# Attention and mixture-of-experts on one core: the dense branch moved into the attention stage, TensorE's order written by hand

## The chip, the cores and the metric

The kernel runs on one core of a Trainium2 chip. The metric is device time in microseconds (us) of one execution, from the first to the last instruction with what lies around it; lower is better. TensorE (PE) runs the matmuls, VectorE (DVE) and ScalarE (ACT) read and write the tiles, GpSimd (POOL) computes squares and issues the DMAs of v, of the weights and of all gathers and scatters, SyncE (SP) issues the other DMAs.

## The reference

```python
# attention: q, k, v of 8 batches x 12 heads x 448 positions x 64
q_n, k_n = rmsnorm(q, g_q), rmsnorm(k, g_k)
attn = softmax(q_n @ k_n.T / 8)          # per head
x = (attn @ v) as (3584 tokens, 768)
# mixture of experts on x, D = 768, E = 8, F = 512
y_dense = relu(x @ w1_dense) @ w2_dense
expert_idx = argmax(x @ w_gate); gate_w = softmax(x @ w_gate)[expert_idx]
y_moe[token] = gate_w * (relu(x @ w1[e]) @ w2[e])   # e = expert_idx[token]
out = y_dense + y_moe
```

## The kernel before

The work has three stages.

**Attention.** A unit of work is a pair of heads (48 pairs, 6 for each batch of 448 tokens). A group of two pairs is loaded at a time: q and k by SP (L132), v by POOL (L140). For each pair POOL squares q and k (L151), DVE sums the squares (L152), ACT makes the reciprocal root (L158, L159) and DVE multiplies (L167). TensorE transposes the result (L177) and DVE copies it out of PSUM (L182, L184). Then TensorE makes the scores of both heads in four score tiles, one for each quarter of the keys (L193), ACT takes the exponentials (L195), TensorE multiplies them with v (L206, 32 matmuls per pair), DVE divides by the sums (L214, L219), TensorE transposes the 448 x 128 result (L227) and ACT copies it to `xT` (L229). After a batch's sixth pair `route` makes the gate logits (L238), the choice of expert on DVE, and two DMAs of the token rows to the DRAM tensor `x_rows` (L258, L259). Meanwhile the weights of the dense branch (`wd`) and of all eight experts (`we`) come in through POOL's queue (L114, L115).

**Routing.** Two matmuls count the tokens of each expert, a chain of DVE instructions (L312 to L390) turns the counts into a sorted list of 35 tiles of 128 slots, each tile of one expert, with a chain of 32 matmuls (L370) in the middle.

**Experts.** For each of the 35 tiles POOL gathers its rows (L397), TensorE transposes them (L407, to `xp`), multiplies them with the expert's first matrix (L414, to `he`) and with the dense branch's first (L420, to `hd`), transposes the expert's hidden values (L426), and adds dense (L432) and expert (L436) products into `yp`; DVE copies `yp` to `ys` (L440) and POOL scatters the rows to `out` (L441).

The order of each engine's instructions is set by a list scheduler that sees the program as written and its data dependences; a tile pool with n buffers lets a producer run n tiles ahead. Matrix tiles in PSUM: two score tiles of two banks, one `av` of two banks, two `tr` of one.

Of the kernel before, what the change touches and what calls it, by code (L numbers as in the profile page):

```python
# [17 lines left out]
def kernel(  # L18
# [89 lines left out]
    nc.gpsimd.dma_start(wgb, moe_w_gate.rearrange("(ko p) e -> p ko e", p=P))  # L108
# [4 lines left out]
    def load_weights(dst1, dst2, s1, s2):  # L113
        nc.gpsimd.dma_start(dst1, s1.rearrange("(ko p) f -> p ko f", p=P))  # L114
        nc.gpsimd.dma_start(dst2, s2.rearrange("(fo p) d -> p fo d", p=P))  # L115

    def load_expert(dst, e):
        load_weights(dst[:, 0].rearrange("p (ko f) -> p ko f", f=F),
                     dst[:, 1].rearrange("p (fo d) -> p fo d", d=Dm), moe_w1[e], moe_w2[e])

    with tc.tile_pool(name="a_ld", bufs=3) as ld, \
         tc.tile_pool(name="a_sb", bufs=2) as sb, \
         tc.tile_pool(name="a_sc", bufs=2, space=bass.MemoryType.PSUM) as scp, \
         tc.tile_pool(name="a_av", bufs=1, space=bass.MemoryType.PSUM) as avp, \
         tc.tile_pool(name="a_tr", bufs=2, space=bass.MemoryType.PSUM) as trp:
        xin, ssqs, rs, xn, qkT, exs, vas, xnats, xTs = {}, {}, {}, {}, {}, {}, {}, {}, {}

        def load(g):
            b, h0 = divmod(g * GP * 2, H)
            for name, src in (("q", q), ("k", k)):  # L130
                t = ld.tile([SC, 2 * GP, JJ * D], F32, tag="x" + name)
                nc.sync.dma_start(  # L132
                    t, src[b, h0:h0 + 2 * GP].rearrange("h (p j) d -> p h (j d)", j=JJ))
                xin[name, g] = t
            ssqs[g] = sb.tile([SC, 2, 2 * GP * JJ], F32, tag="ssq", name="ssq")

        def load_v(g):
            b, h0 = divmod(g * GP * 2, H)
            vr = ld.tile([SC, 2 * GP, JJ * D], BF16, tag="vr", bufs=2)
            nc.gpsimd.dma_start(vr, v[b, h0:h0 + 2 * GP].rearrange("h (p j) d -> p h (j d)", j=JJ))  # L140
            va = ld.tile([SC, 2 * GP, JJ, D + 2], BF16, tag="va")
            nc.vector.memset(va[:, :, :, D:], 1.0)
            nc.vector.tensor_copy(va[:, :, :, :D], vr.rearrange("p h (j d) -> p h j d", d=D))  # L143
            vas[g] = va

        def squares(t):
            g, i = divmod(t, GP)
            for n, name in enumerate("qk"):
# [5 lines left out]
                    sq.rearrange("p h (j d) -> p (h j) d", d=D), AX.X, ALU.add)  # L154

        def rnorm(g):
            r = sb.tile([SC, 2, 2 * GP * JJ], F32, tag="r", name="r")
            nc.scalar.activation(r, ssqs[g], AF.Ln, bias=eps_t[:SC], scale=1.0 / D)  # L158
            nc.scalar.activation(r, r, AF.Exp, scale=-0.5)  # L159
            rs[g] = r  # L160

        def normalise(t):
            g, i = divmod(t, GP)
            for n, name in enumerate("qk"):
# [8 lines left out]
        def transposes(t):  # L173
            for name in "qk":
                ps = trp.tile([P, S], BF16, tag="tr")
                for j in range(JJ):
                    nc.tensor.transpose(ps[:, j * SC:(j + 1) * SC],  # L177
                                        xn[name, t][:, j].rearrange("p h d -> p (h d)"),
                                        ident[:SC, :SC])
                y = sb.tile([P, S], BF16, tag="T" + name)  # L180
                if name == "q":
                    nc.vector.tensor_scalar(y, ps, gqk, None, op0=ALU.mult)  # L182
                else:
                    nc.vector.tensor_copy(y, ps)  # L184
                qkT[name, t] = y

        def scores(t, j):
            if j == 0:
                exs[t] = sb.tile([SC, JJ, 2, S], BF16, tag="ex", name="ex", bufs=2)
# [7 lines left out]
        av = {}  # L197

        def attend(t, part):
            b, pr = divmod(t, NPR)  # L200
            if part == 0:
                av[t] = avp.tile([P, 2, 512], F32, tag="av", name="av")
            hh, m0 = divmod(part * 2, 4)
            for mi in (m0, m0 + 1):
                for j in range(JJ):
                    nc.tensor.matmul(av[t][:, hh, mi * De:(mi + 1) * De],  # L206
                                     exs[t][:, j, hh, QC[mi]:QC[mi] + P],
                                     vas[t // GP][:, 2 * (pr % GP) + hh, j, :De],
                                     start=(j == 0), stop=(j == JJ - 1))

        def divide(t):
            a4 = av[t][:, :, :4 * De].rearrange("p h (m e) -> p h m e", e=De)
            inv = sb.tile([P, 2, 4, 1], F32, tag="inv")
            nc.vector.reciprocal(inv, a4[:, :, :, D:])  # L214
            b, pr = divmod(t, NPR)
            if pr == 0:
                xnats[b] = sb.tile([P, 4, RW], BF16, tag="xa", name="xa", bufs=2)
                xTs[b] = sb.tile([P, NPR, S], BF16, tag="xT", name="xT", bufs=1)
            nc.vector.tensor_mul(  # L219
# [55 lines left out]
        for t in range(2 * GP):  # L275
            norm_ahead(t)
# [205 lines left out]
```

## Time and profile before

| | us |
|---|---|
| median of 3 runs | 606.62 |
| lowest, highest | 598.64, 606.91 |
| the profiled execution | 599.36 |
| its span in the trace | 597.7 |

The profiled execution is 1.2% below the median. The span can be cut by the stage: attention until about 318 us, routing until the first expert tile at about 354 us, the experts until 592 us. Shares of an engine over the whole span mix these stages.

### The profile page before, as it was taken

To read this page: it belongs to the slowest core of one execution; us is meant where nothing else is said; L and a number is where in the kernel's file an instruction comes from. 1 tells how busy PE (TensorE), PEld (TensorE's weight loads), DVE (VectorE), ACT (ScalarE), POOL (GpSimd) and SP (SyncE) were. 2 spreads that over 40 slices of the span, in tenths; PEclk is the share of its full clock that TensorE was granted. 3 is DMA by queue.
4 is the path that set the end of the run, shared out by engine and by line. 5 is a ranking of instruction groups with operands and counts; after the bars stand their busy time and mean duration, and the time that the engine had idled before them with its cause. 6 is when DMAs were issued, how large, how long until landed. Compare 5 with 4: busy or idle time off the path is not lost.

```text
span 597.7 us, 11804 instructions
## 1 busy us (share of the span) xinstructions
PE 443.1 (74%) x4682; PEld 294.6 (49%) x4682; DVE 311.6 (52%) x666; ACT 247.4 (41%) x367; POOL 205.7 (34%) x223
## 2 busy tenths in 40 slices
PE   0558766679986697689781058888889888888895
PEld 0335444445554465456450046556656565555663
DVE  4589976678778768776645513223232322223231
ACT  0447774566676677667780002111121122111220
POOL 5567654336344333542000022222322233222321
PEclk9998985575587858855995559999999999999999
DMA  8999999993654365443101012222122122222210
GB/s 174 222 157 237 239 250 225 230 237 80 148 130 125 82 137 139 78 124 78 47 3 47 0 41 82 71 80 80 64 86 91 65 81 93 90 80 73 81 63 1
DMA packets 55253, 65.89 MB, mean 110 GB/s; under 512 B 4365, under 2 KB 51725, under 8 KB 55200
## 3 DMA queue, kind: packets, MB, share of 16 engines
q0 software_dynamic: 28768, 37.59, 30.2%
q1 hardware_dynamic: 26432, 27.54, 16.5%
q8 instruction: 39, 0.64, 0.4%
q14 instruction: 14, 0.11, 0.1%
HBM read 68.27 MB, written 19.28 MB: 146 GB/s over the span
## 4 chain that ended last, share of the span: by engine, by line
DMA 31%; issue 26%; PE 17%; DVE 15%; POOL 4%; ACT 4%; SPq 1%; POOLq 0%; DVEq 0%; ACTq 0%
DMA out_dram<-ys,dest 16%; DMA vr<-in_v_dram 7%; PE av L206 7%; DMA t<-in_k_dram 5%; PE ps L193 5%; DVE y L167 4%; ACT ex L195 4%; POOL sq L151 3%; PE ps L177 2%; DVE xa L219 2%; DMA t<-in_q_dram 2%; DVE ssq L152 2%; PE ps L227 2%; DVE va L143 1%; POOL xg L397 1%
## 5 line engine op out<-in xcount | busy, mean ns | idle before, releaser
L195 ACT ACTIVATE ex<-ps 112x896 bf16<-112x896 f32 x192 | 168.9, 918 | 67.7 <-PE ps L193 66.5
L151 POOL TENSOR_TENSOR sq<-t 112x512 f32<-112x512 f32 x96 | 101.5, 1074 | 109.1 <-DMA t<-in_q_dram 56.3
L193 PE MATMUL ps<-y 64*112 64x448 bf16 x384 | 98.3, 493 | 41.9 <-DVE y L184 25.9
L206 PEld LDWEIGHTS <-ex 112*128 112x128 bf16 x1536 | 73.6, 114 | 70.8 <-issue 40.4
L206 PE MATMUL av<-va,ex 112*128 112x65 bf16 x1536 | 93.8, 220 | 18.1 <-DVE xa L219 18.0
L416 ACT ACTIVATE hs<-he,xg 128x512 bf16<-128x512 f32 x35 | 24.1, 687 | 183.0 <-PE he L414 183.0
L441 POOL DMA_INDIRECT out_dram<-ys,dest x35 | 35.5, 1016 | 158.7 <-DVE ys L440 158.7
L167 DVE TENSOR_TENSOR y<-t,r 112x512 bf16<-112x512 f32 x96 | 78.7, 843 | 1.6 <-ACT r L159 1.6
L152 DVE TENSOR_REDUCE ssq<-sq 112x8 f32<-112x512 f32 x96 | 62.9, 675 | 26.8 <-POOL sq L151 26.8
L440 DVE COPY ys<-yp 128x768 f32<-128x768 f32 x35 | 33.5, 958 | 77.4 <-PE yp L436 77.4
L432 PE MATMUL yp<-wd,hdT 128*128 128x384 bf16 x280 | 51.6, 327 | 25.8 <-ACT hdT L423 20.0
L397 POOL DMA_INDIRECT xg<-x_rows,row x35 | 34.2, 977 | 86.3 <-DVE dest L390 70.6
L193 PEld LDWEIGHTS <-y 64*112 64x112 bf16 x384 | 30.3, 148 | 64.3 <-DVE y L184 29.4
L177 PE MATMUL ps<-ident,y 112*128 112x112 bf16 x384 | 40.1, 262 | 26.9 <-DVE y L167 24.6
L428 DVE COPY heT<-hp 128x512 bf16<-128x512 bf16 x35 | 14.9, 425 | 85.1 <-PE xp L407 71.5
L420 PEld LDWEIGHTS <-wd 128*128 128x128 bf16 x840 | 51.1, 99 | 8.6 <-issue 0.6
L420 PE MATMUL hd<-xT,wd 128*128 128x128 bf16 x840 | 53.9, 222 | 0.0
L414 PE MATMUL he<-we,xT 128*128 x210 | 52.3, 386 | 0.8 <-DVE xT L409 0.8
L436 PE MATMUL yp<-we,heT 128*128 x280 | 51.2, 326 | 0.0
L432 PEld LDWEIGHTS <-hdT 128*128 128x128 bf16 x280 | 24.5, 98 | 45.3 <-ACT hdT L423 24.6
L177 PEld LDWEIGHTS <-y 112*128 112x128 bf16 x384 | 30.1, 124 | 29.7 <-DVE y L167 25.3
L423 ACT ACTIVATE hdT<-hd 128x512 bf16<-128x512 f32 x35 | 20.9, 597 | 43.3 <-PE xp L407 38.9
(95 smaller groups left out, 392.8 us busy)
## 6 DMA issues: line engine op xcount, KB each, us to landing
we<-in_moe_w_dram POOLq DMA_DIRECT2D x16, 768.0 KB, 29.1
t<-in_q_dram SPq DMA_DIRECT2D x24, 448.0 KB, 5.9
t<-in_k_dram SPq DMA_DIRECT2D x24, 448.0 KB, 7.0
vr<-in_v_dram POOLq DMA_DIRECT2D x24, 224.0 KB, 6.7
x_rows<-xa SPq DMA_DIRECT2D x8, 577.5 KB, 3.7
wd<-in_moe_w_dense_dram POOLq DMA_DIRECT2D x2, 768.0 KB, 10.1
x_rows<-xa SPq DMA_DIRECT2D x8, 96.2 KB, 3.6
xg<-x_rows,row POOLq DMA_INDIRECT x35, 3.1
```

What stands on the lines that cost most here:

```text
L151: nc.gpsimd.tensor_mul(sq, x, x)
L152: nc.vector.tensor_reduce(ssqs[g][:, n, 2 * i * JJ:(2 * i + 2) * JJ], sq.rearrange("p h (j d) -> p (h j) d", d=D), AX.X, ALU.add)
L167: nc.vector.tensor_mul(y.rearrange("p j h d -> p h j d"), x.rearrange("p h (j d) -> p h j d", d=D), rs[g][:, n, 2 * i * JJ:(2 * i + 2) * J ...
L177: nc.tensor.transpose(ps[:, j * SC:(j + 1) * SC], xn[name, t][:, j].rearrange("p h d -> p (h d)"), ident[:SC, :SC])
L193: nc.tensor.matmul(ps[:, hh, :S], qkT["k", t][d0:d0 + D, j * SC:(j + 1) * SC], qkT["q", t][d0:d0 + D, :], start=True, stop=True)
L195: nc.scalar.activation(exs[t][:, j], ps[:, :, :S], AF.Exp, scale=scale)
L206: nc.tensor.matmul(av[t][:, hh, mi * De:(mi + 1) * De], exs[t][:, j, hh, QC[mi]:QC[mi] + P], vas[t // GP][:, 2 * (pr % GP) + hh, j, :De], ...
L397: nc.gpsimd.indirect_dma_start(out=xg, out_offset=None, in_=xd, in_offset=bass.IndirectOffsetOnAxis(ap=row[:, t:t + 1], axis=0))
L414: nc.tensor.matmul(he, xT[:, kk], we[:, bass.ds(ereg, 1), 0, kk * F:(kk + 1) * F].rearrange("p o f -> p (o f)"), start=(kk == 0), stop=(kk ...
L420: nc.tensor.matmul(hd[:, ff], wd1[:, kk, ff * P:(ff + 1) * P], xT[:, kk], start=(kk == 0), stop=(kk == KD - 1))
L432: nc.tensor.matmul(yp[:, dd, :HD], hdT[:, ff], wd2[:, ff, dd * HD:(dd + 1) * HD], start=(ff == 0), stop=False)
L436: nc.tensor.matmul(yp[:, dd, :HD], heT[:, ff], we[:, bass.ds(ereg, 1), 1, ff * Dm + dd * HD:ff * Dm + (dd + 1) * HD] .rearrange("p o f -> ...
```

## The change

Five things change together.

- The **dense branch** leaves the expert tiles. It is computed batch by batch inside the attention loop from `xT`, one batch behind: `dense1` (24 matmuls of 448 columns, ACT's relu after each six) and `dense2` (32 matmuls of 384 columns, copied out by ACT and DVE in turn), cut into 28 pieces that are dealt out over the four quarters of a pair. Its result is written by SP to DRAM beside the token row: the tensor `records` has rows of 1153 floats where `x_rows` had 385. An expert tile gathers the whole record and adds the dense part when it copies `yp` out.
- TensorE's instructions in the attention loop stay in the **order of the program** (`manual_schedule`): one score tile of a quarter, then a transposition or one head of the product with v, then dense pieces. `attend` works on one head, with its own division.
- All PSUM tiles but the scores share one pool of four one-bank buffers.
- q, k and v are loaded three groups ahead, and the weights are a list of jobs issued along the pairs.
- The **expert loop** is written as a software pipeline in TensorE's program order, with two PSUM buffers for `he`, gathers four tiles ahead, and `yp` in one buffer.

```diff
-    xd = nc.dram_tensor("x_rows", (N, RW // 2), F32).ap()
+    RC = RW // 2 + Dm
+    rec = nc.dram_tensor("records", (N, RC), F32).ap()
...
+         tc.tile_pool(name="a_wk", bufs=4, space=bass.MemoryType.PSUM) as wkp:
...
+        def attend(t, hh):
...
+            av = wkp.tile([P, 4, De], F32, tag="wk", name="av")
+            for mi in range(4):
...
+            inv = sb.tile([P, 4, 1], F32, tag="inv")
+            nc.vector.reciprocal(inv, av[:, :, D:])
+            h = 2 * pr + hh
+            nc.vector.tensor_mul(xnats[b][:, :, h * D:(h + 1) * D], av[:, :, :D],
+                                 inv.to_broadcast([P, 4, D]))
...
+        def dense1(b, ff, part, n=3):
+            if part == 0:
+                if ff == 0:
+                    hTs[b] = sb.tile([P, FT, S], BF16, tag="hT", name="hT", bufs=1)
+                ffs[0] = wkp.tile([P, S], F32, tag="wk", name="ff")
+            for kk in range(part * KD // n, (part + 1) * KD // n):
+                nc.tensor.matmul(ffs[0], wd1[:, kk, ff * P:(ff + 1) * P], xTs[b][:, kk],
+                                 start=(kk == 0), stop=(kk == KD - 1))
+            if part == n - 1:
+                nc.scalar.activation(hTs[b][:, ff], ffs[0], AF.Relu)
+
+        def dense2(b, j, dd, part, n=2):
+            if part == 0:
+                if dd == 0:
+                    ffs[1] = sb.tile([SC, 2, Dm // 2], F32, tag="ys", name="ys")
+                ffs[0] = wkp.tile([SC, Dm // 2], F32, tag="wk", name="ff")
+            for ff in range(part * FT // n, (part + 1) * FT // n):
+                nc.tensor.matmul(ffs[0], hTs[b][:, ff, j * SC:(j + 1) * SC],
+                                 wd2[:, ff, dd * Dm // 2:(dd + 1) * Dm // 2],
+                                 start=(ff == 0), stop=(ff == FT - 1))
+            if part == n - 1:
+                if dd == 0:
+                    nc.scalar.copy(ffs[1][:, dd], ffs[0])
+                else:
+                    nc.vector.tensor_copy(ffs[1][:, dd], ffs[0])
+                    r0 = b * S + j * SC
+                    nc.sync.dma_start(rec[r0:r0 + SC, RW // 2:],
+                                      ffs[1].rearrange("p a d -> p (a d)"))
...
+        with tc.manual_schedule(engines={mybir.EngineType.PE}):
...
+            for t in range(NT + NPR):
...
+                for i in range(4):
+                    if t + 1 < NT:
+                        scores(t + 1, i)
+                    if i % 2 == 0:
+                        if t + 2 < NT:
+                            transposes(t + 2, "qk"[i // 2])
+                        if i == 2 and 0 < t <= NT:
+                            xtrans(t - 1)
+                    elif t < NT:
+                        attend(t, i // 2)
+                    dense(t, i)
...
+            ys = sb.tile([P, 2, HD], F32, tag="ys")
+            nc.vector.tensor_add(ys, yp[:, :, :HD],
+                                 xgs[t][:, RW // 2:].rearrange("p (a d) -> p a d", a=2))
...
+        with tc.manual_schedule(engines={mybir.EngineType.PE}):
+            for t in range(2):
+                xtrans(t)
+            gemm1(0)
+            htrans(0)
+            for t in range(NTL):
+                if t + 4 < NTL:
+                    gather(t + 4)
+                if t + 1 < NTL:
+                    gemm1(t + 1)
+                if t + 2 < NTL:
+                    xtrans(t + 2)
+                gemm2(t)
+                if t + 1 < NTL:
+                    htrans(t + 1)
```

In the middle of the attention stage, TensorE goes from the last product with v of one quarter to a transposition of the divided result (`xa`) and to the next score before:

```order
L206 LDWEIGHTS ex
L206 MATMUL av<-va,ex 128x65
L227 LDWEIGHTS xa
L227 MATMUL ps<-ident,xa 128x128
```

and at the same kind of place now, with `hT` the hidden values of the dense branch of the batch before and `wd_128` its second matrix:

```order
L211 LDWEIGHTS ex
L211 MATMUL av<-va,ex 128x65
L276 LDWEIGHTS hT
L276 MATMUL ff<-wd_128,hT 112x384
L276 LDWEIGHTS hT
L276 MATMUL ff<-wd_128,hT 112x384
L198 LDWEIGHTS y
L198 MATMUL ps<-y 112x448
```

Dense matmuls now stand between the product with v and the next scores.

In the expert stage, POOL's queue before, with the semaphores that each instruction waits for (`DMASW` are those of POOL's own DMAs, in rotation):

```order
L441 DMA out_dram<-ys,dest 3584x768 [waits DMASW1_49,DVE_49]
L397 DMA xg<-x_rows,row 128x385 [waits DMASW6_49,Activation_49]
L441 DMA out_dram<-ys,dest 3584x768 [waits DMASW3_49,DVE_49]
L397 DMA xg<-x_rows,row 128x385 [waits DMASW0_49,Activation_49]
L441 DMA out_dram<-ys,dest 3584x768 [waits DMASW5_49,DVE_49]
```

and now:

```order
L487 DMA out_dram<-ys,dest 3584x768 [waits DMASW6_49,DVE_49]
L441 DMA xg<-records,row 128x1153 [waits DMASW1_49,Activation_49]
L487 DMA out_dram<-ys,dest 3584x768 [waits DMASW0_49,DVE_49]
L441 DMA xg<-records,row 128x1153 [waits DMASW3_49,Activation_49]
L487 DMA out_dram<-ys,dest 3584x768 [waits DMASW2_49,DVE_49]
```

The order is the same: scatters and gathers take turns, the gathered rows are three times as long, and a scatter waits for the landing of the scatter before it (`DMASW0`, then `DMASW2`, is the semaphore of the scatter two rows up).

On DVE, between the last batch's routing and the first instruction of the routing stage (`tot`), before:

```order
L256 RECIPROCAL xa<-sm 128x4
L305 MEMSET oh 64x8x4
L312 COPY tot<-tp 128x256
L314 MEMSET onef 128x32
L317 SCALAR_TENSOR_TENSOR incl<-onef,tot 128x32 x8
```

and now:

```order
L253 RECIPROCAL xa<-sm 128x4
L349 MEMSET oh 64x8x4
L283 COPY ys<-ff 112x384 x4
L356 COPY tot<-tp 128x256
L358 MEMSET onef 128x32
L361 SCALAR_TENSOR_TENSOR incl<-onef,tot 128x32 x8
```

The last batch's dense results now stand ahead of the routing stage.

## Rows read from the trace of the kernel before

**Rows 1.** Busy time by stage: window, length, each engine's busy (instructions), clock, DMA, GB/s.

```profile
0.00:130.00 130.00, 78.18 (x874) 49.62 (x874) 95.17 (x214) 70.31 (x104) 72.61 (x89) 0.83 1.12 219
130.00:300.00 170.00, 136.89 (x1607) 89.55 (x1607) 125.38 (x288) 119.84 (x177) 63.35 (x64) 0.70 0.47 108
318.00:354.00 36.00, 4.11 (x39) 3.55 (x40) 16.98 (x39) 0.00 (x0) 2.99 (x3) 0.50 0.12 36
358.00:592.00 234.00, 206.99 (x1934) 140.54 (x1931) 66.90 (x104) 44.27 (x69) 65.31 (x66) 1.00 0.22 75
```

**Rows 2.** TensorE in order of time, one expert tile: start, length, instruction.

```profile
444.88 1.50 PE L420 MATMUL hd<-xT,wd 128*128 128x128 bf16 x24
446.22 0.39 PE L426 MATMUL hp<-ident,hs 128*128 128x128 bf16 x4
446.44 0.50 PE L407 MATMUL xp<-ident,xg 128*128 128x128 bf16 x6
447.77 1.48 PE L432 MATMUL yp<-wd,hdT 128*128 128x384 bf16 x8 [0.83 <-issue]
449.08 1.46 PE L436 MATMUL yp<-we,heT 128*128 x8
450.38 1.46 PE L414 MATMUL he<-we,xT 128*128 x6
```

**Rows 3.** POOL in order of time: the scatters of two neighbouring tiles.

```profile
445.02 1.02 POOL L441 DMA_INDIRECT out_dram<-ys,dest  x1 [4.49 <-DVE ys L440]
451.81 1.02 POOL L441 DMA_INDIRECT out_dram<-ys,dest  x1 [4.50 <-DVE ys L440]
```

**Rows 4.** The scatters' tile view: from issue to landing.

```profile
DMA to landing us min/median/max: 2.1/3.1/3.1
```

**Rows 5.** TensorE in order of time, one pair to the next at the lower clock.

```profile
262.46 1.06 PE L206 MATMUL av<-va,ex 112*128 112x65 bf16 x16
268.16 1.06 PE L206 MATMUL av<-va,ex 112*128 112x65 bf16 x16 [0.17 <-DVE xa L219]
```

**Rows 6.** The same at the higher clock, late, with no preparation of q and k left.

```profile
304.83 0.64 PE L206 MATMUL av<-va,ex 112*128 112x65 bf16 x15
...
308.14 0.40 PE L193 MATMUL ps<-y 64*112 64x448 bf16 x2 [0.32 <-ACT ex L195]
308.52 0.68 PE L206 MATMUL av<-va,ex 112*128 112x65 bf16 x16
```

**Rows 7.** L206 alone by window: 32 matmuls are one pair; then clock, DMA, GB/s.

```profile
0.00:130.00 130.00, 31.27 (x496) 0.83 1.12 219
130.00:300.00 170.00, 56.53 (x912) 0.70 0.47 108
192.00:205.00 13.00, 3.57 (x74) 1.00 0.41 89
230.00:243.00 13.00, 3.50 (x72) 1.00 0.43 90
```

**Rows 8.** Busy time as in Rows 1, in two stretches of one clock each.

```profile
254.00:284.00 30.00, 27.48 (x276) 18.00 (x272) 21.86 (x53) 20.66 (x30) 10.43 (x11) 0.50 0.42 101
230.00:243.00 13.00, 8.37 (x119) 5.24 (x118) 9.83 (x24) 9.48 (x14) 5.62 (x6) 1.00 0.43 90
```

**Rows 9.** The chain that ended last, between attention and routing: start, length, what.

```profile
313.53 0.70 DVE xa L219
...
317.65 3.66 DMA x_rows<-xa
```

**Rows 10.** TensorE, the first expert tile's first product, at the lower clock.

```profile
353.70 2.72 PE L414 MATMUL he<-we,xT 128*128 x6 [0.82 <-DVE xT L409]
```

**Rows 11.** DMA of the first 130 us: volume, and `x_rows`: count, KB each, us to landing.

```profile
DMA packets 29221, 28.49 MB, mean 219 GB/s; under 512 B 1962, under 2 KB 29211, under 8 KB 29211
...
x_rows<-xa SPq DMA_DIRECT2D x2, 577.5 KB, 11.0
```

**Rows 12.** The page's costliest groups: busy, mean ns of one, idle before.

```profile
L440 DVE COPY ys<-yp 128x768 f32<-128x768 f32 x35 | 33.5, 958 | 77.4 <-PE yp L436 77.4
...
L423 ACT ACTIVATE hdT<-hd 128x512 bf16<-128x512 f32 x35 | 20.9, 597 | 43.3 <-PE xp L407 38.9
```

More of the change, by code (lines that the diff above doesn't have):

```diff
@@ L128, in load @@
         def load(g):
+            if g * GP >= NT:
+                return
             b, h0 = divmod(g * GP * 2, H)
+            parts = ((0, 2), (2, 4)) if g == 0 else ((0, 2 * GP),)
             for name, src in (("q", q), ("k", k)):
[L131 to L134, printed above, removed]
+                xin[name, g] = ld.tile([SC, 2 * GP, JJ * D], F32, tag="x" + name, name="x" + name)
@@ L135, in load, with values @@
+            for a, z in parts:
+                for name, src in (("q", q), ("k", k)):
+                    nc.sync.dma_start(
+                        xin[name, g][:, a:z],
+                        src[b, h0 + a:h0 + z].rearrange("h (p j) d -> p h (j d)", j=JJ))
+            vr = ld.tile([SC, 2 * GP, JJ * D], BF16, tag="vr")
+            nc.gpsimd.dma_start(vr, v[b, h0:h0 + 2 * GP].rearrange("h (p j) d -> p h (j d)", j=JJ))
+            vrs[g] = vr
             ssqs[g] = sb.tile([SC, 2, 2 * GP * JJ], F32, tag="ssq", name="ssq")
[L137 to L140, printed above, removed]
+        def values(g):
@@ L154, in squares, with normalise @@
                     sq.rearrange("p h (j d) -> p (h j) d", d=D), AX.X, ALU.add)
[L156 to L162, printed above, removed]
+            if i == GP - 1 and "k" in names:
+                r = sb.tile([SC, 2, 2 * GP * JJ], F32, tag="r", name="r")
+                nc.scalar.activation(r, ssqs[g], AF.Ln, bias=eps_t[:SC], scale=1.0 / D)
+                nc.scalar.activation(r, r, AF.Exp, scale=-0.5)
+                rs[g] = r
+        def normalise(t, names="qk"):
             g, i = divmod(t, GP)
-            for n, name in enumerate("qk"):
+            for name in names:
+                n = "qk".index(name)
                 x = xin[name, g][:, 2 * i:2 * i + 2, :]
@@ new lines, with dense @@
+        ffs = [None, None]
+        PIECES = [(dense1, ff, p) for ff in range(FT) for p in range(3)] + \
+                 [(dense2, j, dd, p) for j in range(JJ) for dd in range(2) for p in range(2)]
+        NSL = 4 * NPR - 2
+        def dense(t, i):
+            b, pr = divmod(t, NPR)
+            n = 4 * pr + i - 2
+            if b > 0 and n >= 0:
+                for f, *args in PIECES[n * len(PIECES) // NSL:(n + 1) * len(PIECES) // NSL]:
+                    f(b - 1, *args)
+        with tc.manual_schedule(engines={mybir.EngineType.PE}):
+            for g in range(3):
+                load(g)
+            for job in wjobs[:3]:
+                nc.gpsimd.dma_start(*job)
+            for t in range(2 * GP):
+                squares(t)
+            values(0)
+            for t in range(3):
+                normalise(t)
+            for t in range(2):
+                transposes(t, "q")
+                transposes(t, "k")
@@ L422, in ffn @@
-            hdT = sb.tile([P, FT, P], BF16, tag="hdT")
-            nc.scalar.activation(hdT, hd, AF.Relu)
-            hp = ps1.tile([P, FT, P], BF16, tag="tr")
-            for ff in range(FT):
-                nc.tensor.transpose(hp[:, ff], hs[:, ff * P:(ff + 1) * P], ident)
-            heT = sb.tile([P, FT, P], BF16, tag="heT")
-            nc.vector.tensor_copy(heT, hp)
+                nc.tensor.matmul(he, xTs[t][:, kk],
+                                 we[:, bass.ds(eregs[t], 1), 0, kk * F:(kk + 1) * F]
+                                 .rearrange("p o f -> p (o f)"),
+                                 start=(kk == 0), stop=(kk == KD - 1))
@@ L444, in ffn @@
                 bounds_check=N - 1, oob_is_err=False)
[L446 removed]
+        eregs = {}
+        for t in range(4):
             gather(t)
[L448 to L451 removed]
+        with tc.manual_schedule(engines={mybir.EngineType.PE}):
+            for t in range(2):
+                xtrans(t)
[11 more added lines that the diff above has]
+                    htrans(t + 1)
 _INS = ['q', 'k', 'v', 'g_q', 'g_k', 'moe_w_gate', 'moe_w1_dense', 'moe_w2_dense', 'moe_w1', 'moe_w2']
```

192 lines of the change are left out of this document (76 added, 116 removed).

## The prediction

> **What bounds the kernel now.** I read the busy time by stage first, since the shares over the whole span mix three different limits [rows 1]. In the expert stage TensorE is busy 207.0 of 234 us at the full clock, and no other engine comes near 30%: that stage is TensorE's. In the attention stage it changes at about 130 us. Until then the DMA share stands at 1.12, which is as full as it gets, and 28.49 MB move at 219 GB/s [rows 1, 11]: all expert weights come in here beside q, k and v, and only 496/32 = 15.5 pairs get done, 8 us each [rows 7]. From 130 to 300 us the DMA share is 0.47; 912/32 = 28.5 pairs take 170 us, 5.96 us each, with TensorE busy 136.9, DVE 125.4 and ACT 119.8 us, at a mean clock of 0.70 [rows 1, 7].
>
> The 0.70 is a mixture of the two levels, 1.2 and 2.4 GHz. At 1.2 GHz one pair follows the other in 268.16 - 262.46 = 5.70 us with TensorE almost without a gap [rows 5], and in one such stretch of 30 us it is busy 27.48 [rows 8]: TensorE is the bound. At 2.4 GHz it needs 308.52 - 304.83 - 0.32 of wait = 3.37 us for a pair [rows 6]; yet with the preparation of later pairs going on beside it, pairs take 13/(74/32) = 5.6 and 13/(72/32) = 5.8 us, and TensorE is busy only 8.37 of 13 us, DVE 9.83, ACT 9.48 [rows 7, 8]: a chain of waits through all engines, with none of them full. Routing is a chain of 36 us in which TensorE does next to nothing [rows 1].
>
> **The expert stage.** A tile's period is 451.81 - 445.02 = 6.79 us [rows 3]. From start to start on TensorE [rows 2] the removed parts are L420 (446.22 - 444.88 = 1.34 us), L432 (449.08 - 447.77 = 1.31 us) and the wait of 0.83 us ahead of it for the dense hidden values. What stays is the first product, 1.29 us (as L414 before L420: 6 x 512 columns at L436's rate, 8 x 384 in 450.38 - 449.08 = 1.30), L436 at 1.30, four transpositions in 446.44 - 446.22 = 0.22 and six in 0.33: 3.14 us. The new order puts each product's successor far enough away: ACT's relu and copy (0.6 us each by L423) and DVE's copy of `xT` have a product of 1.3 us to hide behind. The one `yp` buffer must be emptied by the add (0.96 us, as L440 [rows 12]) within the 0.22 + 1.29 + 0.33 = 1.84 us until the next L436, which holds with 0.9 us to spare; if DVE came that much late, the excess would be paid in every tile.
>
> The next in line is POOL's scatter. It waits for the landing of the one before, which comes 3.1 us after its issue, and 2.1 us for a tile without tokens [rows 4]; before, 6.79 us hid that, now it is the neighbour of 3.14. With the wait's own reaction I take 3.2 to 3.3 for that chain. POOL itself has a gather and a scatter of 1.0 us each, which fit. The gather grows from 1540 to 4612 bytes a row; a scatter carries 393 KB in the 1.0 us by which a full one is later than an empty one, so a gather of 590 KB costs about 1.5 us of transfer. Both together are 2.5 us of DMA in a period, which still fits. TensorE and the scatters can trip over each other, so I take 3.4 us for a tile, between 3.2 and 4.2 (a scatter that shares the engines with the larger gather lands up to 1 us later). The stage changes by 35 x (3.4 - 6.79) = -119 us (-126 to -91).
>
> **The attention stage.** TensorE gets per batch 24 matmuls of 448 columns and 32 of 384. At L420's rate, 1.34/24 = 0.056 us for 128 columns, one of the first costs 0.195 us; at L432's, 1.31/8 = 0.164. That is 4.7 + 5.2 = 9.9 us a batch, 1.65 a pair, at 2.4 GHz, and double that at 1.2 (L414's six in 2.51 us on the first tile [rows 10], against 1.29). A pair then needs 3.37 + 1.65 = 5.0 us of TensorE at the high clock and 5.7 + 3.2 = 8.9 at the low one. ACT does 119.84/28.5 = 4.2 us a pair now and gets four relus (0.5 to 0.6 us, L423 [rows 12]) and four copies (about 0.5) per batch: +0.7. DVE does 4.4 and gets four copies a batch (+0.3) and a second reciprocal with the division cut in two (about +0.3): 5.0. So all three come to 4.9 to 5.0 us. That they were only some 75% full before came from waits for loads and for each other; loads three groups ahead and the interleaving take part of those away. I take 5.7 us a pair at the high clock (5.2 if the waits vanish), and for the clock a seventh of the time at 1.2 GHz, so 6.2 us a pair: 28.5 x (6.2 - 5.96) = +7 us. The last four pairs, which took 3.7 us [rows 6], now need the 5.0 of TensorE: +5. SP's added writes of the dense rows are 11 MB over the whole stage, where the DMA share after 130 us is 0.47: hidden; ahead of 130 us only one or two batches' rows (1.4 MB each, 6 us at 219 GB/s) come on top, and there the pairs wait for the same weights and loads as before, so I leave that phase at its 130 us, plus or minus 8. Cutting the division, sharing PSUM buffers and the finer loads cost nothing that is not in these sums.
>
> The clock is the largest unknown. The trace shows both: TensorE busy 27.48 of 30 us and still at 1.2 GHz [rows 8], and 234 us at 2.4 GHz under dense products [rows 1]. I take a seventh because the dense products fill the gaps after which it fell. The Trainium skill, "TensorE: Matmul & The Clock Gate", section "What's actually happening", says that the slow clock is the default and that recent activity releases it. Taken by itself that would leave almost no time at 1.2 GHz and a pair at 5.7, which gives 488 us for the whole; the 30 us of [rows 8] speak against it.
>
> **Between the stages.** The last batch's dense branch has no pairs left to hide in. Its 9.9 us of TensorE follow the last routing logits, its last results pass through DVE ahead of `tot`, and a row buffer waits for a DMA of 3.7 us. Before, `tot` waited 3.66 us for `x_rows` [rows 9], which this takes the place of: +10 us (+8, or +20 at the low clock). The routing chain itself stays.
>
> **Sum** on the profiled execution's 599.4 us: -119 + 12 + 10 = **502 us**. The median of the runs is 1.2% above that execution; I don't add it.
>
> **The rivals.**
> - *The low clock keeps its share.* With 60% of the time at 1.2 GHz, as the mean of 0.70 says for now, a pair takes 0.4 x 5.7 + 0.6 x 8.9 = 7.6 us, +40: about 543. For it: the clock stayed low under 92% busy. Against it: dense products replace the gaps. Chance 0.13.
> - *The scatter chain lengthens.* DMAs did land late when the engines were full: `x_rows` took 11.0 us in the first 130 us [rows 11], against 3.66 later [rows 9]. With 4.3 us a tile, +31: 533. Against it: 2.5 us of transfer in 3.4. The Trainium skill, "DMA: Bandwidth & Descriptors", section "Latency and other measured facts", gives HBM's latency as 0.2 us on average and 2 us at high load; by that the estimate for a tile would be some 5 us and for the whole some 560. Chance 0.10.
> - *All waits give way.* A pair at 5.3, a tile at 3.2: 502 - 26 - 7 = 469. Chance 0.09.
> - *TensorE never leaves 1.2 GHz in attention.* From the first dense piece on, at pair 6, pairs take 8.9 us where 8 was DMA's pace: +9 until pair 16, then 32 x 8.9 = 285 us against 183.5 from 130 to 313.5, +101, and +20 for the last batch: 599 - 119 + 130 = 610, and 620 or more with the scatters at 3.7. This is **slower** than before; it decides when the mean pair exceeds 5.96 + 109/32 = 9.4 us. A mean clock of 0.70 with less work argues against so pure a case. Chance 0.04.
> - *No change.* The written order makes TensorE wait in each quarter for ACT's exponential two tiles back and for DVE, so that pairs take some 9 us at any clock: about 595. Chance 0.04.
>
> **How the numbers follow.** The forecast has the remaining 0.60. Its own range is 480 to 525: a pair between 5.7 and 6.6 us, a tile between 3.2 and 3.7. To hold 8 in 10 the range must reach the first two rivals, and nearly the third: 470 to 548. All but the last two cases are faster by far more than 2%, which is about what a measurement of this kernel can tell from no change: faster 0.92, within 2% 0.04, slower 0.04.
>
> **What would show it.** In the profile after: an expert tile's scatters 3.4 us apart, the chain there running through the scatters' landings rather than through TensorE alone; a pair every 6 us between 130 and 300 us at a mean clock near 0.93; some 16 pairs by 130 us; the first expert product about 22 us later than at 353.7. A mean clock of 0.7 or less in that stretch, or tiles above 4 us, would prove those steps wrong. A stall of TensorE's fixed order that no row here shows would make the whole wrong.

## The result, and the profile after

The changed kernel takes 540.51 us (median of 4 runs, 538.08 to 541.91) where the kernel before takes 606.76 (598.64 to 610.52): a ratio of 0.894, with a 95% interval of 0.885 to 0.904. The ratios to the kernel before, here and below, leave out runs in a slower state of the chip; the medians hold all runs. The forecast of 502 us was too fast by 38 us. Its range of 470 to 548 holds the time; the likeliest case's own range, 480 to 525, does not. The profiled execution took 539.3 us, its span 537.3.

Busy time by stage after the change, with the columns of [rows 1]:

```profile
0.00:130.00 130.00, 82.69 (x866) 48.30 (x866) 90.64 (x233) 67.59 (x105) 69.46 (x86) 0.83 1.14 230
130.00:300.00 170.00, 149.50 (x1738) 84.88 (x1736) 133.94 (x346) 127.10 (x203) 68.15 (x67) 0.94 0.57 139
300.00:336.00 36.00, 35.03 (x453) 21.18 (x453) 21.05 (x61) 29.75 (x45) 0.00 (x0) 1.00 0.25 77
400.00:500.00 100.00, 80.30 (x557) 45.27 (x567) 35.63 (x48) 30.02 (x48) 47.74 (x48) 0.98 0.67 219
```

The clock in the second row rose from 0.70 to 0.94, as forecast. In the last row, inside the expert stage, TensorE is busy only 80% of the time at the full clock, where it had been busy 207 of 234 us. That stage is no longer TensorE's.

The products with v alone, in the same two windows (32 matmuls are one pair; they stand in L211 now, and answer to [rows 7]):

```profile
0.00:130.00 130.00, 23.32 (x448) 0.83 1.14 230
130.00:300.00 170.00, 37.66 (x848) 0.94 0.57 139
```

That is 14.0 pairs by 130 us (15.5 before) and 26.5 from there to 300 (28.5 before), 6.4 us each. The 7.5 left are done by 335.5 us, in 4.7 us each. The ends of the attention and the start of the experts, as groups with first and last start:

```profile
L217 DVE TENSOR_TENSOR xa<-av,inv x15: 416/424/427, 301.2 to 335.5; 128x256 bf16<-128x256 f32 x15
...
L461 PE MATMUL he<-we,xT x31: 376/379/631, 382.2 to 399.9; 128*128 x31
```

The last division starts at 335.5 us instead of 313.53 [rows 9], 22 us later. The first expert product starts at 382.2 instead of 353.70 [rows 10], 28.5 later. What lies between grew from 40.2 to 46.7 us.

POOL in order of time in the expert stage (the square bracket is the idle time before an instruction and what ended it), which answers to [rows 3]:

```profile
441.35 1.02 POOL L487 DMA_INDIRECT out_dram<-ys,dest  x1 [1.60 <-DMA out_dram<-ys,dest]
442.68 0.97 POOL L441 DMA_INDIRECT xg<-records,row  x1 [0.30 <-issue]
445.10 1.02 POOL L487 DMA_INDIRECT out_dram<-ys,dest  x1 [1.45 <-DVE xT L454]
...
455.46 1.02 POOL L487 DMA_INDIRECT out_dram<-ys,dest  x1 [1.59 <-DMA out_dram<-ys,dest]
456.78 0.97 POOL L441 DMA_INDIRECT xg<-records,row  x1 [0.30 <-issue]
459.34 1.02 POOL L487 DMA_INDIRECT out_dram<-ys,dest  x1 [1.59 <-DVE xT L454]
```

The scatters' own view, with their number, their first and last start, and at the end the landing, which answers to [rows 4]:

```profile
L487 POOL DMA_INDIRECT out_dram<-ys,dest x35: 982/1022/1042, 391.0 to 531.8; - x35
...
DMA to landing us min/median/max: 3.1/4.4/4.7
```

A tile takes (531.8 - 391.0)/34 = 4.14 us on the mean; before, the mean was (592.0 - 363.7)/34 = 6.72. Where nothing else is late, two scatters stand 459.34 - 455.46 = 3.88 us apart, and the next one waits for the landing of the last ("DMA out_dram" in the bracket). Where the bracket names DVE's copy of another tile (L454), the scatter doesn't need it: a wait is put down to the signal that came last by the records, and its 1.45 to 1.6 us are the same wait.

The mean of 4.14 is a mixture. Of the 34 intervals between scatters 25 are 3.90 us or shorter, and nine lie between 4.56 and 6.47, as this one of 433.56 - 428.14 = 5.42 us:

```profile
428.14 1.02 POOL L487 DMA_INDIRECT out_dram<-ys,dest  x1 [1.04 <-DVE xT L454]
429.47 0.97 POOL L441 DMA_INDIRECT xg<-records,row  x1 [0.30 <-issue]
433.56 1.02 POOL L487 DMA_INDIRECT out_dram<-ys,dest  x1 [3.12 <-DVE ys L485]
```

The view's landings rest on eight scatters, seven of them late ones, so its median of 4.4 us is not that of the stage. The trace also keeps the moments at which the DMAs raise their semaphores. By these, 25 of the 34 scatters that another one follows land within 3.1 us, and nine, those ahead of the long intervals, after 3.75 to 4.72; the median is 3.08. In 32 of the 34 intervals the next scatter starts 0.76 to 0.81 us after the landing: POOL's waiting instruction ends 0.03 to 0.04 us after it, and the scatter starts 0.73 to 0.77 us after that.

The three differences make up the whole: +22 in attention, +6.5 between the stages, and for the experts, from the first product to the end of the span, (537.3 - 382.2) - (597.7 - 353.7) = -89. That is -60.5; the profiled executions differ by 539.3 - 599.4 = -60.1.

### The profile page after: what moved, and what is told of

It is laid out like the page before. It is cut to its first block, busy times and chain, and to the rows that moved or that the text cites. A ratio compares the mean times of both kernels' runs of the same rounds, so it can differ in the third digit from the quotient of the medians.

```text
span 537.3 us, 10725 instructions
## 1 busy us (share of the span) xinstructions
PE 401.6 (75%) x3995; PEld 232.5 (43%) x4010; DVE 319.0 (59%) x759; ACT 273.8 (51%) x431; POOL 207.1 (39%) x223
## 5 line engine op out<-in xcount | busy, mean ns | idle before, releaser
L157 POOL TENSOR_TENSOR sq<-xq 112x512 f32<-112x512 f32 x48 | 50.8, 1058 | 84.0 <-DMA xq<-in_q_dram 51.9
L211 PE MATMUL av<-va,ex 112*128 112x65 bf16 x1536 | 71.2, 202 | 11.5 <-DVE xa L217 8.7
L276 PE MATMUL ff<-wd,hT 128*112 128x384 bf16 x256 | 62.4, 356 | 15.8 <-DVE xa L217 15.6
L211 PEld LDWEIGHTS <-ex 112*128 112x128 bf16 x1536 | 59.1, 103 | 34.0 <-issue 20.7
L441 POOL DMA_INDIRECT xg<-records,row x35 | 33.9, 968 | 91.7 <-DVE dest L434 81.3
L487 POOL DMA_INDIRECT out_dram<-ys,dest x35 | 35.7, 1019 | 79.4 <-DVE ys L485 28.5
L157 POOL TENSOR_TENSOR sq<-xk 112x512 f32<-112x512 f32 x48 | 54.0, 1125 | 30.1 <-DMA xk<-in_k_dram 15.4
L454 DVE COPY xT<-xp 128x768 bf16<-128x768 bf16 x35 | 19.5, 558 | 73.8 <-PE xp L452 69.8
L182 PE MATMUL tr<-ident,y 112*128 112x112 bf16 x384 | 39.7, 233 | 27.1 <-DVE y L173 24.5
L473 ACT COPY heT<-hp 128x512 bf16<-128x512 bf16 x35 | 20.5, 585 | 69.3 <-PE hp L471 69.3
L466 ACT ACTIVATE hs<-he,xg 128x512 bf16<-128x512 f32 x35 | 24.1, 687 | 62.3 <-DMA xg<-records,row 35.5
L198 PEld LDWEIGHTS <-y 64*112 64x112 bf16 x384 | 26.5, 132 | 63.1 <-issue 51.2
L265 PE MATMUL ff<-xT,wd 128*128 128x448 bf16 x192 | 50.6, 367 | 2.6 <-DVE xa L217 2.6
L485 DVE TENSOR_TENSOR ys<-yp,xg 128x768 f32<-128x768 f32 x35 | 33.5, 958 | 28.9 <-PE yp L479 28.9
L173 DVE TENSOR_TENSOR y<-xq,r 112x512 bf16<-112x512 f32 x48 | 42.5, 886 | 0.8 <-ACT r L164 0.7
L452 PE MATMUL xp<-ident,xg 128*128 128x128 bf16 x210 | 18.6, 228 | 31.5 <-DMA xg<-records,row 23.4
```

Source lines behind the costliest of these rows:

```text
L157: nc.gpsimd.tensor_mul(sq, x, x)
L173: nc.vector.tensor_mul(y.rearrange("p j h d -> p h j d"), x.rearrange("p h (j d) -> p h j d", d=D), rs[g][:, n, 2 * i * JJ:(2 * i + 2) * J ...
L182: nc.tensor.transpose(ps[:, j * SC:(j + 1) * SC], xn[name, t][:, j].rearrange("p h d -> p (h d)"), ident[:SC, :SC])
L198: nc.tensor.matmul(ps[:, hh, :S], qkT["k", t][d0:d0 + D, j * SC:(j + 1) * SC], qkT["q", t][d0:d0 + D, :], start=True, stop=True)
L211: nc.tensor.matmul(av[:, mi], exs[t][:, j, hh, QC[mi]:QC[mi] + P], vas[t // GP][:, 2 * (t % GP) + hh, j, :De], start=(j == 0), stop=(j == ...
L265: nc.tensor.matmul(ffs[0], wd1[:, kk, ff * P:(ff + 1) * P], xTs[b][:, kk], start=(kk == 0), stop=(kk == KD - 1))
```

## The experiments

All times are whole-kernel times; where the table says "single", it is one run, the others are medians of four. Each kernel is the changed one with the edit shown. The table gathers what was read from each trace in the same way as above.

| kernel | us | pairs by 130 us | pairs 130 to 300 | last division | first expert product | us per tile |
|---|---|---|---|---|---|---|
| changed | 540.5 | 14.0 | 26.5 | 335.5 | 382.2 | 4.14 |
| two targets (single) | 521.9 | 13.5 | 26.3 | 339.9 | 386.5 | 3.41 |
| short gather (single) | 536.8 | 13.5 | 26.0 | 342.4 | 386.7 | 3.89 |
| TensorE free in attention | 530.6 | 14.5 | 28.0 | 326.1 | 372.2 | 4.12 |
| GpSimd in order too | 523.6 | 17.0 | 26.4 | 321.4 | 368.0 | 4.10 |
| GpSimd in order, TensorE free | 528.3 | 16.2 | 27.0 | 323.5 | 369.6 | 4.05 |
| the same, two targets (single) | 503.3 | 16.5 | 27.0 | 321.0 | 367.3 | 3.43 |
| no dense branch (single) | 482.0 | 16.5 | 31.5 | 299.7 | 334.1 | 3.83 |
| TensorE free in the expert loop (single) | 541.2 | 14.0 | 26.5 | 336.6 | 387.3 | 4.04 |
| one expert's weights | 520.2 | 17.5 | 26.5 | 316.8 | 363.2 | 4.07 |
| one expert's weights, TensorE free | 511.1 | 16.5 | 28.5 | 313.0 | 358.8 | 4.02 |
| weights held back by data | 539.8 | 16.5 | 23.5 | 338.3 | 384.5 | 4.06 |

Four of these kernels have the same attention stage, with all weights and both orders as in the changed kernel: their last divisions lie between 335.5 and 342.4 us. A difference below 7 us in that column is no finding. The kernels were also timed on several chips: the kernel before, run beside them, took 607.4 us (median) beside the four that follow the changed one, 602.2 beside the next four, and 600 to 602 beside the last three. So a difference of some 5 us between these groups isn't one either.

### Odd tiles to a second target

```diff
-                out=out, out_offset=...
+                out=(out, out2)[t % 2], out_offset=...
```

> The changed kernel with every odd tile scattered to a second DRAM tensor, so that a scatter waits for the scatter two tiles back and not for the last one; the odd tiles' rows are missing from the output. In the changed kernel 34 scatter intervals take 140.8 us, 4.14 us a tile, with landings 4.4 us after issue. If the wait for the landing before is the bound, a tile falls to 3.3 to 3.5 us, TensorE's 3.14 and its trips, and the time by 22 to 28 us, to about 514. If the transfers' volume is the bound (207 GB/s, share 0.63, gathers three times as large landing late), a tile stays at 3.9 to 4.2 and the time at 532 to 541.

A scatter now waits for the last but one. The expert stage of this run, busy time from 400 to 500 us, and its scatters to both targets:

```profile
400.00:500.00 100.00, 94.09 (x685) 56.14 (x695) 43.67 (x59) 36.53 (x58) 57.78 (x58) 1.00 0.83 271
```

```profile
L487 POOL DMA_INDIRECT out_dram<-ys,dest x18: 985/1022/1042, 397.5 to 513.3; - x18
L487 POOL DMA_INDIRECT out_odd<-ys,dest x17: 985/1022/1027, 400.6 to 510.8; - x17
```

35 tiles start within 513.3 - 397.5 us, 3.41 each: the 3.4 of the prediction, with TensorE busy 94% again and 271 GB/s through the DMA engines. So neither TensorE nor the larger gather keeps a tile from 3.4 us; the wait for the landing of the scatter ahead does. It costs 0.73 us a tile, 25 us in the stage. The whole gained 19 us against the median, since the attention stage of this run happened to end 4 us later.

### A gather of the token row alone

The token rows have a tensor of their own again, the gather fetches 1540 bytes a row, and the dense part is not added (it is computed and written, but missing in the output).

```diff
-                out=xg, out_offset=None, in_=rec,
+                out=xg, out_offset=None, in_=xr,
...
-            nc.vector.tensor_add(ys, yp[:, :, :HD], xgs[t][:, RW // 2:]...)
+            nc.vector.tensor_copy(ys, yp[:, :, :HD])
```

> The changed kernel with the token rows in a tensor of their own again, so that an expert tile gathers 1540 bytes a row and not 4612; the dense part is still computed and written to DRAM but is missing from the output, and the add becomes a copy. If the larger gather is what delays the scatters' landing, landings return to 3.1 us and a tile to 3.2 to 3.4: about 512. If the chain of scatters takes 4.1 us whatever the gather, or TensorE's own order does, a tile stays near 4.1: about 538.

Three scatters of this run in POOL's order, and the landings:

```profile
434.94 1.02 POOL L487 DMA_INDIRECT out_dram<-ys,dest  x1 [1.58 <-DMA out_dram<-ys,dest]
...
438.82 1.02 POOL L487 DMA_INDIRECT out_dram<-ys,dest  x1 [1.58 <-DVE ys L486]
...
442.72 1.02 POOL L487 DMA_INDIRECT out_dram<-ys,dest  x1 [1.60 <-DVE ys L486]
```

```profile
DMA to landing us min/median/max: 2.1/3.1/5.3
```

536.81 us, between the two theories. The period is 3.88 and 3.90 us, and 3.89 on the mean of the stage. The landing is 3.1, yet the period is not the expected 3.2 to 3.4: a chain of landing and next scatter lasts some 0.8 us longer than the landing. Only two scatters land later than 3.3 us after their issue (3.65 and 5.28), where nine do with the whole record, so the larger gather makes landings late. It is worth 4.14 - 3.89 = 0.25 us a tile, 9 us in all, by this single run; the other kernels of the table with the whole record and one target take 4.02 to 4.12, which makes it 0.13 to 0.23. In the changed kernel TensorE's transpositions wait for it, the costliest groups from 400 to 500 us say (after the bar: busy time, mean ns, idle time before them and what ended it):

```profile
L452 PE MATMUL xp<-ident,xg 128*128 128x128 bf16 x144 | 12.5, 224 | 18.8 <-DMA xg<-records,row 18.4 <-issue 0.4
L452 PEld LDWEIGHTS <-xg 128*128 128x128 bf16 x144 | 8.5, 99 | 30.1 <-DMA xg<-records,row 29.6
```

Most of this idle time costs nothing, since TensorE would wait for the scatters anyway: with the same gather and two targets it was busy 94%.

### TensorE's attention order left to the scheduler

```diff
-        with tc.manual_schedule(engines={mybir.EngineType.PE}):
+        if True:
             for g in range(3):
```

> The changed kernel with TensorE's attention order left to the scheduler again, the written order kept in the expert loop alone. If the written order only interleaves what would run in any order and the dense products are what holds the clock, the attention stage ends within 6 us of where it did (last pair's division near 335 us) at a clock above 0.9 between 130 and 300 us: 533 to 546. If the written order is what keeps TensorE supplied, pairs take 6.8 us or more and the clock falls to 0.8 or less: 555 to 575.

530.62 us (526.82 to 531.97; 0.881 of the kernel before, 0.868 to 0.894): 10 us faster than the changed kernel, which neither theory had expected. 28.0 pairs instead of 26.5 are done from 130 to 300 us, at a clock of 0.97 instead of 0.94. Fewer waits of TensorE don't explain it: it is idle for 20.5 us of that stretch with the written order (170 - 149.50) and for 20.3 without (170 - 149.75). The gain goes with the clock; whether the order holds the clock down is not tested.

### GpSimd's attention instructions in program order too

```diff
-        with tc.manual_schedule(engines={mybir.EngineType.PE}):
+        with tc.manual_schedule(engines={mybir.EngineType.PE, mybir.EngineType.Pool}):
             for g in range(3):
```

> The changed kernel with POOL's attention instructions kept in the program's order too, so that the 16 expert weight loads are issued one every two and a half pairs up to pair 38 and not all within the first 18. If the weights crowd out q, k and v in the first 130 us (14.2 pairs there, a stall of TensorE of 12.5 us at 83 us behind a load of v), 17 or more pairs get done by 130 us and the whole ends 8 to 16 us sooner: 523 to 531. If the volume only moves to later and delays pairs there, or POOL's fixed order holds the squares back, the time stays within 4 us of 539 or gets longer.

523.6 us (520.48 to 526.27; 0.869 of the kernel before, 0.857 to 0.881), the lowest median of a version with the whole computation. Where the 17 us come from is seen in the first 130 us. The changed kernel's weight loads there, and its waits from 60 to 130 us:

```profile
we<-in_moe_w_dram POOLq DMA_DIRECT2D x16, 768.0 KB, 33.5
```

```profile
PE ff L276 <- DVE xa L217: 12.5, 1, 12.5
POOL we L321 <- DMA we<-in_moe_w_dram: 11.1, 4, 5.0
...
DVE va L148 <- DMA vr<-in_v_dram: 9.1, 1, 9.1
```

The two long waits are one event, as DVE in order of time shows:

```profile
85.13 0.17 DVE L215 RECIPROCAL inv<-av 128x4 f32<-128x4 f32 x1
85.26 0.09 DVE L147 MEMSET va<- 112x32 bf16 x1
94.47 0.43 DVE L148 COPY va<-vr 112x1024 bf16<-112x1024 bf16 x1 [9.12 <-DMA vr<-in_v_dram]
94.81 0.42 DVE L217 TENSOR_TENSOR xa<-av,inv 128x256 bf16<-128x256 f32 x1
```

A load of v lands late; DVE stands at its copy for 9.12 us, with the division (L217) queued behind it; and TensorE, whose next instruction in the written order is a dense matmul into the PSUM buffer that this division must empty first, stands for 12.5 us. At 8 us a pair that is a pair and a half.

With GpSimd in order, from 0 to 130 us:

```profile
DMA packets 27005, 25.61 MB, mean 197 GB/s; under 512 B 2062, under 2 KB 26321, under 8 KB 26993
...
we<-in_moe_w_dram POOLq DMA_DIRECT2D x8, 768.0 KB
```

The program deals out the weights along the pairs, but only TensorE's order was fixed: the scheduler moved all 16 expert loads ahead of 130 us, as it had in the kernel before, which also has 16 there. With 8 of them there the long stall is gone, and 17.0 pairs are done instead of 14.0. The stall of 10 to 12.5 us stands in all four kernels with the changed attention stage. It is not in those with TensorE free, with GpSimd in order, with one expert's weights or without the dense branch: it takes the crowd of weights, the dense pieces and the written order together.

### Both: GpSimd in order, TensorE free, without and with the second target

```diff
-        with tc.manual_schedule(engines={mybir.EngineType.PE}):
+        with tc.manual_schedule(engines={mybir.EngineType.Pool}):
             for g in range(3):
```

> In the attention loop GpSimd's instructions, not TensorE's, stay in program order; TensorE's are left to the scheduler. If the two costs are separate (weights that crowd out q, k and v ahead of 130 us, about -17 us with GpSimd's order; TensorE's written order, about -10 us without it), they add up: 512 to 517 us, some 17 pairs by 130 us and 28 from 130 to 300. Rival: both runs took the same slack (a pair that waits for its loads also waits in the written order), so the second step gives nothing more: 521 to 528, 26 to 27 pairs from 130 to 300.

528.31 us (0.882 of before, 0.869 to 0.894), with 16.2 and 27.0 pairs: the rival. The two gains don't add up.

> The kernel before this one in this call, and odd expert tiles are scattered to a second DRAM tensor, so the output lacks them. If the wait for the landing of the scatter ahead is all that keeps a tile from 3.4 us, tiles go from 4.1 to 3.4 us and the time is 24 to 26 us under the kernel without this edit. Rival: the gathers, issued by the same engine, take over: 3.7 to 3.9 us a tile, 8 to 14 us less.

503.3 us with tiles of 3.43 instead of 4.05: the scatters' wait is worth 0.6 us a tile, some 21 us, in this version also, and the gathers don't take over.

### No dense branch at all

```diff
-            if b > 0 and n >= 0:
+            if False:
```

together with the short gather.

> The dense branch is left out altogether (its output lacks y_dense), and the token rows are gathered alone, as in the run with the short gather. If the dense products are what keeps TensorE at 2.4 GHz, the mean granted clock from 130 to 300 us falls back to 0.7 to 0.8 and pairs there take 5.6 to 6.0 us: attention ends at 315 to 325 us, the first expert product comes 36 to 40 us later, and with 3.9 us a tile the time is 497 to 510 us. Rival: the clock is high because of the interleaving, whatever the products: 0.9 or more, pairs of 4.9 to 5.3 us, attention to 290 to 300, about 472 to 485 us.

Busy time by stage without the dense branch, and L211's products (L212 in this kernel) in the same windows:

```profile
0.00:130.00 130.00, 90.13 (x931) 56.73 (x932) 95.70 (x249) 74.73 (x109) 72.12 (x89) 0.73 1.15 227
130.00:300.00 170.00, 145.74 (x1732) 94.72 (x1729) 142.68 (x363) 127.42 (x187) 66.68 (x66) 0.70 0.45 103
```

```profile
0.00:130.00 130.00, 31.97 (x528) 0.73 1.15 227
130.00:300.00 170.00, 55.52 (x1008) 0.70 0.45 103
```

The clock falls back to 0.70, just as before the change: the dense products keep TensorE at 2.4 GHz, not the interleaving. (How they do it isn't shown: TensorE's idle time in that stretch is 24.3 us without them and 20.5 with them.) But the pairs come every 5.4 us even so, and the time is the rival's. So without dense work the new attention loop is faster than the old one (5.96) by about half a microsecond a pair at the same mean clock. The run also prices the dense branch in its new place: 540.5 - 482.0 = 58 us. Of these, 36 lie in attention (335.5 against 299.7), 12 between the stages (46.7 against 34.4), and 0.31 x 34 = 11 in the tiles. In its old place it took 1.34 + 1.31 + 0.83 = 3.48 us of each of 35 tiles, 122 us of TensorE. Not all of that could be gained, since the scatters hold a tile at 3.83 us even without it: (6.72 - 3.83) x 34 = 98 us are what the tiles became shorter, with the loop's other changes.

### TensorE free in the expert loop

```diff
-        with tc.manual_schedule(engines={mybir.EngineType.PE}):
+        if True:
             for t in range(2):
```

> TensorE's order in the expert loop is left to the scheduler; the loop's text, buffers and gathers stay. If the scatters set the pace, TensorE's order there is worth nothing: tiles of 4.0 to 4.3 us, 533 to 545 us as a whole. Rival: the written pipeline is what brought the tile under 5 us: without it the products wait for relu and copies, 4.8 to 5.5 us a tile, 563 to 590 us.

541.16 us, 4.04 us a tile: TensorE's written order in the expert loop is worth nothing while the scatters set the pace. (That the loop's text, with its buffers and its gathers four ahead, is what brought the products together isn't tested by this.)

### One expert's weights, with TensorE's order written and free

```diff
-    for e in range(E):
+    for e in range(1):
         wjobs.append(...)
```

and every tile multiplied with them.

> The changed kernel with the weights of one expert alone loaded, and every tile multiplied with them (its output leaves out the other seven experts): 11.0 MB less through GpSimd's queue ahead of 130 us; both written orders stay. If those loads are what holds the first phase at 14.0 pairs, pairs there come near the 6.4 us of the phase after: 18 to 20 pairs by 130 us, the last division at 300 to 312 us, and the time is 22 to 35 us under 539. Rival: the first phase is slow because of the low clock and the filling of the pipeline, whatever the loads: 14 to 15.5 pairs, 530 to 540 us. Pairs between 130 and 300 us tell whether the loads matter there too: 26 to 27 if not, 29 or more if so.

517.71 us, with 17.3 and 27.4 pairs and the last division at 315.3: near the first theory, but short of each of its numbers (18 pairs, 312 us, 22 us gained). All that the other weights cost is some 20 us, and the order of GpSimd's instructions alone gave 17. After 130 us the loads matter little: 6.2 us a pair. The same kernel in rounds, beside the version with TensorE free in attention, on the same chip:

> The kernel with one expert's weights alone (its output leaves out the other seven experts), with both written orders, timed in rounds as the partner of the next one: 514 to 521 us, 17 pairs by 130 us and 27 to 28 from 130 to 300.

> The same with one expert's weights alone, and TensorE's order in the attention loop left to the scheduler. If the written order costs TensorE waits by itself, some 10 us go here as they did under the full load of weights: 504 to 511 us, 28.5 pairs or more from 130 to 300. Rival: the order costs only where loads come late, since a fixed order hands each late tile on to all that follows; without the crowd of weights it makes no difference: 514 to 522 us, 27 to 28 pairs from 130 to 300.

520.23 us (518.61 to 525.74) with the order, 511.13 (508.97 to 514.82) without: 9 us again, with 28.5 pairs instead of 26.5 from 130 to 300 us, though one pair fewer ahead of it. So the written order costs time also where weights are not crowded. That it does so in the attention loop is less sure than the 9 us: the last divisions of the two profiled executions lie 3.8 us apart, and the first of the two runs of the same kernel had 27.4 pairs where this one has 26.5. The clock differs here too, 0.94 with the order and 0.98 without.

### Weights held back by data, both orders free

A copy of one element of a finished pair to the weight's tile stands ahead of each load, so that the scheduler can't move it to the front; TensorE is free in attention.

```diff
+                        nc.vector.tensor_copy(wjobs[nw][0][:1, 0, :1],
+                                              xnats[pb][:1, 0, pp * P:pp * P + 1])
                         nc.gpsimd.dma_start(*wjobs[nw])
```

> TensorE's order in the attention loop is left to the scheduler and GpSimd's too, but every weight load is preceded by a copy of one element of a finished pair to its tile, so that it can't start before that pair is done. If the two costs add (weights ahead of 130 us some 14 to 20 us, the written order some 9), 508 to 516 us with 16.5 to 18 pairs by 130 us and 28 or more from 130 to 300. Rival: spread weights take from the later phase what they give in the first one, as in the run with GpSimd's written order and TensorE's free one: 26.5 to 27 pairs from 130 to 300 and 523 to 530 us.

539.81 us (0.896 of before, 0.888 to 0.904), slower than even the rival. The first phase did gain, with 16.5 pairs, but only 23.5 pairs follow by 300 us. In both phases POOL stands at these loads, waiting for the copy; here from 130 to 300 us:

```profile
POOL we L324 <- DVE we L322: 14.4, 4, 5.2
```

v and the squares of later pairs are queued behind it on POOL, and DVE waited 35.5 us there for squares, where it waited 21.9 with TensorE free and no such copies.

## Why the prediction missed by 38 us

**The expert stage, -119 forecast, -89 measured.** The step that failed is the period of the scatter chain. The prediction saw that POOL's scatter, waiting for the one before, is next in line, and took "3.2 to 3.3 for that chain", landing 3.1 with 0.1 to 0.2 for the wait's reaction. It measures 3.88 for a full tile, with the landing of 3.1 as taken: the reaction is 0.8 us, and by the semaphores' records it lies on POOL, after the landing. [Rows 4] gave the landing, and no row gave the rest, since a wait for DVE stood there [rows 3]; so the upper bound belonged here, not a value close to the lower. The remaining 0.25 us go with the large gather: nine of 34 landings come 0.7 to 1.65 us late, where "up to 1 us" had been allowed for. The prediction's own sign against this step, "tiles above 4 us", came true. A smaller slip is that it took 6.79 us off for every tile, where the mean before was 6.72. The rest of the step holds: freed of the chain, a tile took 3.41 us with TensorE busy 94% of the time, near the 3.14 of the sum. Of the rivals this is "the scatter chain lengthens" in size (4.3 forecast), but mostly not by its reason: late landings make the 0.25, not the 0.6 below it. The Trainium skill, "DMA: Bandwidth & Descriptors", section "Latency and other measured facts", gives HBM's latency as 0.2 us on average and 2 us at high load. At the stage's DMA share of 0.67 the trace has landings up to 1.65 us later than usual, but only nine of 34 are late, and the tile stayed at 4.14, under the some 5 us of the estimate by that page.

**The attention stage, +12 forecast, +22 measured.** The clock was right (0.94 against 0.93), and so was its cause, the dense products: without them it is 0.70. (That they do it by filling gaps isn't shown.) The last pairs were right, 4.7 us with TensorE busy 35.03 of 36. Two terms were off. The first 130 us were left unchanged, with "some 16 pairs", because pairs there "wait for the same weights and loads as before"; 14.0 came, after 15.5. The weights were the same, all 16 loads in front in both kernels. New is the stall of 12.5 us, in which one late load of v stops DVE, and by the written order TensorE too. The prediction ended on "a stall of TensorE's fixed order that no row here shows", and gave it no term in the sum. Spreading the weights removes it and gave 14 us in the last division (335.5 to 321.4). The other term is the written order itself, put at nothing: it costs 9 to 10 us in two pairs of kernels (in the first of them the two terms overlap, since freeing TensorE also removes the stall). The rival that gave it a price named waits of TensorE in each quarter, but after 130 us TensorE is idle as long without the order as with it. A pair between 130 and 300 us took 6.4 us instead of 6.2 with it, and 6.1 without (170/28.0).

**Between the stages, +10 forecast, +6.5 measured** against before, and 12 against the same kernel without dense work. Its direction and mechanism hold; what the sum didn't have is that this stretch without dense work is 5.8 us shorter than before (34.4 against 40.2).

**The other rivals.** The clock didn't stay low; that the time came near the 543 us of that rival is chance. Nothing ended above the time before. "All waits give way" needs the scatters' wait gone, which no version with all of the output had.

**What stays open.** Why the written order's 9 to 10 us vanish when GpSimd is in order too (523.6 with TensorE's order, 528.3 without) was not settled; in both, pairs after 130 us take 6.3 to 6.4 us while the held-back weights come in. Why the clock is lower with the written order was not tested. What POOL does in the 0.8 us between a landing and the next scatter isn't in the records. A version whose scatters don't wait for one another and whose output is whole was not tried.

## What to carry to other kernels

When a stage's bound is about to fall to a third or half, list the chains that its length has hidden, and price each by its full period from start to start; where the trace shows only a part of it, keep the forecast in the middle of the bounds. A written order on one engine binds that engine alone: look at where the other engines' queues put the transfers that the order was meant to pace, and what one late transfer stops. And work whose leaving made one stage 98 us shorter may cost 58 in another with idle time, and not nothing.

## What the runs showed of the hardware

Of scatters to one tensor, each waiting for the one before, the next starts 0.76 to 0.81 us after the landing, whatever the landing took (32 of 34 intervals of the changed kernel): 3.88 us from start to start with a landing of 3.07, and 2.86 with one of 2.1; two such streams in turn came to 3.41 us a tile with 271 GB/s moving. TensorE was busy 145.7 of 170 us at a mean clock of 0.70 without the dense products and 149.5 of 170 at 0.94 with them: the busy share of a stage didn't tell which of the two levels was granted. Without the weights of seven experts (168 GB/s in the first 130 us instead of 230), 3.3 to 3.5 pairs more were done there, and no more.
